# A transformer block on one core: zero products as TensorE warm-up, one weight cast moved to GpSimd, and the first input tile loaded by two queues

## The chip, the core and the metric

The kernel runs on one core of a Trainium2 chip. The metric is the device time of one execution in microseconds (us), the median of several runs. Five engines work side by side, each in the order of its own queue: TensorE (PE, with its weight loads as PEld), VectorE (DVE), ScalarE (ACT), GpSimd (POOL) and SyncE (SP, which here only issues transfers). They wait for each other through semaphores. [...]

## The reference

One pre-LayerNorm transformer block in float32, with S = 2048 tokens, D = 512, 32 heads of 16, and F = 1792:

```
h   = x + A(layernorm(x))
out = h + B(layernorm(h))
A: qkv = x @ wqkv; each token attends to itself and 7 earlier tokens, 2 apart; softmax; @ wo
B: relu(x @ w1 + b1)**2 @ w2 + b2
```

## The kernel before

Matrix products are made in three parts. Every float32 operand is split into a high part (a rounding copy to the type float32r, function `hi`, on ScalarE, or `hi_T` for an activation) and a low part (source minus high part, function `lo`, on VectorE or GpSimd). `mm3` then adds high x high, low x high and high x low in one PSUM bank, 4 k-blocks each, so 12 products.

The first stage makes q, k and v. Tokens come in 16 tiles of 128 rows (`xt`), and the weight matrix `wqkv` in 4 column groups `gp` of 4 row blocks `k` (128x384 each, `wraw` as loaded). The first sixteen slots of the main loop take tiles t = 0 to 3 with each group in turn. Tile t is centred by `x_center` (three VectorE instructions: statistics, their sum, subtraction), transposed by four TensorE instructions (`x_T`, `transposes`, L201), then ScalarE makes its high part `xh` out of PSUM and VectorE its low part `xl` (`lo_T`). In slot t the four high x high products come first, then tile t+1's transposes, then the other eight products (L228). For t = 0 these eight are `xl` by `big_h`, then `xh` by `big_l`; for later tiles the other way round. `big_h` and `big_l` hold the high and low parts of the weights, and `rs` is each row's inverse deviation, which GpSimd makes and ScalarE applies when it copies a result out of PSUM (L526).

The order is written by hand: the kernel schedules nothing by itself. Chores are put down for a slot (`at`, `after`) and emitted there. What stands ahead of the loop is this:

- GpSimd fills the identity matrix `ident` and a few constants (L931 to L937).
- SyncE issues tile 0, tile 1, `wraw` rows k = 2 and 3, tiles 2 and 3 and the other groups; ScalarE issues `wraw` rows k = 0 and 1, since `load_wqkv(0, (0, 1), nc.scalar)` names its queue.
- TensorE transposes `ident` by itself 18 times into a PSUM bank that nobody reads (L949 to L951).
- `x_center(0)`, `x_center(1)`, the high parts of rows k = 0 and 1 on ScalarE (`hi_wqkv`), tile 0's transposes, the high parts of k = 2 and 3, then the low parts: k = 1 and 2 on GpSimd, k = 0 and 3 on VectorE, `x_rstd` on GpSimd, and `x_center(2)`.

After this stage come attention on VectorE and GpSimd, the output projection and the MLP, which the change doesn't touch. `wo_h` holds weights that are first written much later.

## Time and profile before

| what | us |
|---|---|
| median of 3 runs | 504.56 (504.14 to 506.01) |
| the profiled execution, own time | 504.66 |
| its span, first to last instruction | 502.8 |
| TensorE busy in the span | 496.9 (99%) |
| VectorE, ScalarE, GpSimd busy | 378.2, 302.2, 353.4 |

The profiled execution's time is 0.10 us above the median of the runs. Times in the rows count from the span's start. A row of a timeline says start, duration, engine, line, operation, output and inputs, and how many like ones were merged; in brackets stands what the engine waited for. [...]

### The profile page before, as it was taken

How to read it: one execution, taken by the hardware profiler on the slowest of the kernel's cores; microseconds unless marked ns; L12 is line 12 of the kernel's file. 1: busy time of each engine (PE TensorE's matmuls, PEld its weight loads, DVE VectorE, ACT ScalarE, POOL GpSimd, SP SyncE). 2: the span in 40 equal slices, each digit the busy share in tenths (PEclk: the TensorE clock that was granted, in tenths of full speed). 3: DMA queues.
4: the chain of work that ended last, by engine and by line, in shares of the span. 5: the costliest groups of instructions: out<-in, count | busy, mean ns of one | idle time of the engine just before them, and what ended most of it. 6: DMA issues, size and time to landing. Idle time of an engine off the chain costs nothing.

```text
span 502.8 us, 7520 instructions
## 1 busy us (share of the span) xinstructions
PE 496.9 (99%) x2414; PEld 422.6 (84%) x2414; DVE 378.2 (75%) x524; ACT 302.2 (60%) x540; POOL 353.4 (70%) x430
## 2 busy tenths in 40 slices
PE   8999999999999999999999999999999999999997
PEld 7999888888888888888888888888888888998986
DVE  6379899988989989788879998888984255833233
ACT  4635777768346758368564555755554958766541
POOL 5614798886685999969877877769799363786610
PEclk9999999999999999999999999999999999999999
DMA  8678989889798988679576856966654556355112
GB/s 263 188 226 212 315 249 302 285 255 283 219 190 277 303 277 256 201 215 260 179 253 198 222 151 187 234 207 239 219 158 71 127 164 188 112 162 167 64 42 86
DMA packets 111472, 103.15 MB, mean 205 GB/s; under 512 B 31560, under 2 KB 79944, under 8 KB 111432
## 3 DMA queue, kind: packets, MB, share of 16 engines
q1 hardware_dynamic: 110488, 102.14, 69.2%
q10 hardware_dynamic: 944, 0.52, 0.3%
q8 instruction: 19, 0.31, 0.3%
q14 instruction: 21, 0.17, 0.1%
HBM read 72.65 MB, written 24.25 MB: 193 GB/s over the span
## 4 chain that ended last, share of the span: by engine, by line
PE 95%; DVE 1%; issue 1%; POOL 1%; DMA 1%; ACT 0%; POOLq 0%; DVEq 0%
PE mm L228 49%; PE acc L899 28%; PE wo L228 9%; PE mm L822 7%; PE tr L201 2%; DMA xt<-in_A_x_dram 1%; POOL tl L155 1%; DVE s L757 0%; PE half L922 0%; POOL rl L155 0%; POOL h L679 0%; DVE s L758 0%; DVE big_l L155 0%; ACT big_l L152 0%; DVE st L457 0%
## 5 line engine op out<-in xcount | busy, mean ns | idle before, releaser
L408 POOL TENSOR_TENSOR pr<-pr 128x512 f32<-128x512 f32 (+1 forms) x128 | 133.6, 1044 | 35.0 <-DVE pr L351 29.6
L228 PE MATMUL mm<-big_l,w_h 128*128 128x512 f32 x336 | 88.4, 389 | 0.0
L351 DVE TENSOR_TENSOR pr<-ex,v 128x1024 f32<-128x1024 f32 x64 | 78.0, 1220 | 13.7 <-POOL o L408 9.0
L340 DVE TENSOR_TENSOR pr<-qp,k 128x1024 f32<-128x1024 f32 x64 | 76.8, 1200 | 10.7 <-ACT qp L268 7.3
L374 DVE TENSOR_REDUCE ex<-pr 128x64 f32<-128x1024 f32 x64 | 78.5, 1226 | 2.0
L228 PEld LDWEIGHTS mm<-big_l,w_h 128*128 128x128 f32 x336 | 63.0, 188 | 13.4 <-issue 0.3
L155 POOL TENSOR_TENSOR rl<-r,rh 128x512 fp32r<-128x512 f32 x42 | 55.3, 1320 | 25.5 <-ACT rh L152 25.4
L228 PE MATMUL mm<-big_l,xh 128*128 128x512 f32 (+1 forms) x208 | 55.9, 379 | 0.0
L228 PE MATMUL mm<-big_h,xh 128*128 128x512 f32 (+1 forms) x208 | 53.7, 380 | 0.7 <-ACT xh L152 0.7
L228 PE MATMUL mm<-big_h,xl 128*128 128x512 f32 (+1 forms) x208 | 53.0, 377 | 0.0
L899 PE MATMUL acc<-big_h,rh 128*128 128x512 f32 x190 | 52.0, 391 | 0.0
L899 PE MATMUL acc<-big_l,rh 128*128 128x512 f32 x190 | 52.0, 390 | 0.0
L899 PE MATMUL acc<-big_h,rl 128*128 128x512 f32 x190 | 51.7, 389 | 0.0
L228 PE MATMUL mm<-big_l,w_l 128*128 128x512 f32 x168 | 44.9, 389 | 0.0
L228 PEld LDWEIGHTS mm<-big_h,xh 128*128 128x128 f32 x208 | 38.4, 190 | 6.5 <-ACT xh L152 1.1
L228 PEld LDWEIGHTS mm<-big_h,xl 128*128 128x128 f32 x208 | 38.9, 191 | 5.9
L899 PEld LDWEIGHTS acc<-big_h,rl 128*128 128x128 f32 x190 | 35.7, 188 | 7.4
L899 PEld LDWEIGHTS acc<-big_l,rh 128*128 128x128 f32 x190 | 35.6, 188 | 7.5
L228 PEld LDWEIGHTS mm<-big_l,xh 128*128 128x128 f32 x208 | 37.4, 188 | 4.9
L899 PEld LDWEIGHTS acc<-big_h,rh 128*128 128x128 f32 x190 | 35.0, 188 | 6.7
L875 ACT ACTIVATE r<-mm,b_sb 128x512 f32<-128x512 f32 x42 | 28.8, 685 | 15.3 <-PE mm L228 14.6
L528 ACT COPY y<-mm 128x512 f32<-128x512 f32 x36 | 21.1, 586 | 26.7 <-PE mm L228 24.2
(160 smaller groups left out, 918.9 us busy)
## 6 DMA issues: line engine op xcount, KB each, us to landing
k<-qkv_d SPq DMA_DIRECT2D x48, 288.0 KB, 3.6
v<-qkv_d SPq DMA_DIRECT2D x48, 288.0 KB, 3.5
qkv_d<-y SPq DMA_DIRECT2D x18, 512.0 KB, 4.1
big_l<-w2l_d SPq DMA_DIRECT2D x24, 256.0 KB, 3.1
xt<-in_A_x_dram SPq DMA_DIRECT2D x16, 256.0 KB, 4.4
q<-qkv_d SPq DMA_DIRECT2D x32, 128.0 KB, 3.3
h<-in_A_x_dram SPq DMA_DIRECT2D x16, 256.0 KB, 3.6
h_d<-h SPq DMA_DIRECT2D x16, 256.0 KB, 2.8
```

The source lines that it names most:

```text
L155: eng.tensor_tensor(out=dst, in0=src, in1=h, op=ALU.subtract)
L201: nc.tensor.transpose(tr[:, k, :], src[:, k * P:(k + 1) * P], ident)
L228: nc.tensor.matmul(ps, l(k), r(k), start=(n == 0), stop=(n == 3 * KB - 1))
L340: nc.vector.tensor_tensor(out=pr.rearrange("p i w h d -> p i w (h d)"), in0=qps["now"][:, j % 2].unsqueeze(2).to_broadcast([P, RI, W, GC]) ...
L351: nc.vector.tensor_tensor(out=p2, in1=vwin, op=ALU.mult, in0=e1[:, :, :, j * GH:(j + 1) * GH].unsqueeze(4).to_broadcast([P, RI, W, GH, DH]))
L374: nc.vector.tensor_reduce(out=lf[:, :, :, j * GH:(j + 1) * GH], in_=pr, axis=X, op=ALU.add)
L408: nc.gpsimd.tensor_tensor(out=dst, in0=p2[:, :, :w], in1=p2[:, :, w:2 * w], op=ALU.add)
L528: nc.scalar.copy(dst, src)
L822: nc.tensor.matmul(ps, sta[y][:, k], mov[x][:, k], start=(first and q == 0), stop=(last and q == len(terms) - 1), skip_group_check=True)
L875: nc.scalar.activation(r, ps, AF.Relu, bias=b1_sb[:, f:f + 1])
L899: nc.tensor.matmul(acc[j], l[:, j * P:(j + 1) * P], w[f], start=(first and n < len(js)), stop=(last and n >= len(terms) - len(js)))
```

## The change

Four edits, all ahead of the main loop:

1. VectorE fills `blank`, the first 128x128 corner of `wo_h`, with zeros, and TensorE multiplies `blank` by itself 21 times (float32r, 128 columns) in place of the 18 transposes of `ident`.
2. Three more such products stand between tile 0's transposes and its first real product.
3. The high part of weight row k = 1 of group 0 is made by GpSimd.
4. Tile 0 is loaded as two transfers of 64 rows, one issued by SyncE, one by ScalarE ahead of its two weight rows.

```
-WARM = 18
+WARM = 21, 3
...
-    def hi_wqkv(gp, k):
-        hi(pair(wq_h, k, gp), raws[gp, k])
+    def hi_wqkv(gp, k, copy=nc.scalar.copy):
+        copy(pair(wq_h, k, gp), raws[gp, k])
...
+    blank = wo_h[:, 0, :P]
+    nc.vector.memset(blank.bitcast(F32), 0.0)
     make_identity(nc, ident)
...
-    load_x(0)
+    xt[0] = row("xt")
+    for n, eng in enumerate((nc.sync, nc.scalar)):
+        half = slice(n * P // 2, (n + 1) * P // 2)
+        eng.dma_start(xt[0][half], x_v[0, 0, 0, half])
     load_wqkv(0, (0, 1), nc.scalar)
...
-    for n in range(WARM):
-        nc.tensor.transpose(warm[:, n % KB, :], ident, ident)
+    def keep_busy(count):
+        for n in range(count):
+            nc.tensor.matmul(warm[:, n % KB, :], blank, blank, start=True, stop=True)
+
+    keep_busy(WARM[0])
...
     hi_wqkv(0, 0)
-    hi_wqkv(0, 1)
+    hi_wqkv(0, 1, nc.gpsimd.tensor_copy)
...
     x_T(0)
+    keep_busy(WARM[1])
     run(due)
```

On TensorE, from its first instruction to the first product, the order changes so (- before, + now; `tr` is the PSUM bank, `mm` the first product's bank):

```order
-L951 MATMUL tr<-ident 128x128 x18
-L201 MATMUL tr<-ident,xt 128x128 x4
+L958 MATMUL tr<-wo_h 128x128 x21
+L201 MATMUL tr<-ident,xt 128x128 x4
+L958 MATMUL tr<-wo_h 128x128 x3
 L228 MATMUL mm<-big_h,xh 128x384 x4
```

The warm-up is of another kind, and three of it stand behind the transposes; nothing else moves on TensorE in the whole program.

On ScalarE, before, from its first transfer to the casts behind tile 0's `xh`:

```order
L562 DMA wraw<-in_A_wqkv_dram 128x3x128 x2
L152 ACT_TABLE_LOAD
L152 CAST big_h<-wraw 128x3x128 x2
L152 CAST xh<-tr 128x512
L152 CAST big_h<-wraw 128x3x128 x2
```

And now:

```order
L944 DMA xt<-in_A_x_dram 64x512
L562 DMA wraw<-in_A_wqkv_dram 128x3x128 x2
L565 ACT_TABLE_LOAD
L565 CAST big_h<-wraw 128x3x128
L152 CAST xh<-tr 128x512
L565 CAST big_h<-wraw 128x3x128 x2
```

One transfer has come in ahead of the weight rows, and one cast of a weight row instead of two stands ahead of `xh`.

On GpSimd, behind the constants, now:

```order
L938 AFFINE_SELECT mask<-mask 128x32
L565 CAST big_h<-wraw 128x3x128
L155 TENSOR_TENSOR big_l<-wraw,big_h 128x3x128 x2
L465 TENSOR_SCALAR rs_154<-mv_153 128x1
L467 TENSOR_TENSOR rs_154<-rs_154,mhalf 128x1
```

The cast is new there; before, the two low parts (L155) followed the mask directly.

## Rows read from the trace of the kernel before

**Rows 1.** Waits of PE in the whole span: us in total, times, longest.
```profile
PE mm L228 <- ACT xh L152: 0.7, 1, 0.7
PE mm L822 <- DVE wo_l L155: 0.5, 1, 0.5
```
**Rows 2.** The chain that ended last, first 30 us: start, us, what.
```profile
0.72 3.40 DMA xt<-in_A_x_dram
...
4.15 0.70 DVE st L457
...
6.79 0.59 ACT xh L152
...
7.42 1.65 PE mm L228 x4
9.07 0.85 PE tr L201 x4
...
12.45 0.44 PE tr L201 x4
```
**Rows 3.** Timeline of PEld, first 16 us.
```profile
1.34 3.71 PEld L951 LDWEIGHTS tr<-ident 128*128 128x128 f32 x18 [1.34 <-POOL ident masks.py:199]
...
9.51 1.19 PEld L228 LDWEIGHTS mm<-big_h,xl 128*128 128x128 f32 x4
10.69 0.71 PEld L228 LDWEIGHTS mm<-big_l,xh 128*128 128x128 f32 x4
```
**Rows 4.** Timeline of PE, first 16 us.
```profile
5.63 1.11 PE L201 MATMUL tr<-ident,xt 128*128 128x128 f32 x4 [0.19 <-DVE xt L459]
...
8.87 1.05 PE L201 MATMUL tr<-ident,xt 128*128 128x128 f32 x4
...
11.57 0.87 PE L228 MATMUL mm<-big_h,xh 128*128 128x384 f32 x4
12.28 0.60 PE L201 MATMUL tr<-ident,xt 128*128 128x128 f32 x4
```
**Rows 5.** Timeline of ACT, first 16 us.
```profile
5.30 1.15 ACT L152 CAST big_h<-wraw 128x384 fp32r<-128x384 f32 x2 [1.96 <-DMA wraw<-in_A_wqkv_dram]
6.79 0.59 ACT L152 CAST xh<-tr 128x512 fp32r<-128x512 f32 x1 [0.34 <-PE tr L201]
7.27 0.93 ACT L152 CAST big_h<-wraw 128x384 fp32r<-128x384 f32 x2
```
**Rows 6.** Timeline of SP, first 16 us: its issues of transfers.
```profile
0.72 0.87 SPq L439 DMA_DIRECT2D xt<-in_A_x_dram  x2
1.64 1.34 SPq L562 DMA_DIRECT2D wraw<-in_A_wqkv_dram  x2
```
**Rows 7.** Transfers, first 20 us: issues, KB each, median us to landing.
```profile
wraw<-in_A_wqkv_dram SPq DMA_DIRECT2D x14, 192.0 KB, 4.3
```
**Rows 8.** Transfer queues (q1 SyncE's, q10 ScalarE's), 2.4 to 2.9 us: packets, MB, share.
```profile
q1 hardware_dynamic: 34, 0.06, 57.6%
q10 hardware_dynamic: 2, 0.00, 0.6%
```
**Rows 9.** Timeline of POOL, first 16 us: two low parts of weight rows.
```profile
6.53 2.33 POOL L155 TENSOR_TENSOR big_l<-wraw,big_h 128x384 fp32r<-128x384 f32 x2 [4.75 <-DMA wraw<-in_A_wqkv_dram]
```
**Rows 10.** Timeline of DVE, first 20 us.
```profile
8.01 1.74 DVE L155 TENSOR_TENSOR big_l<-wraw,big_h 128x384 fp32r<-128x384 f32 x2
9.67 0.68 DVE L457 BATCH_NORM_STATS2 st<-xt 128x6 f32<-128x512 f32 x1
...
10.60 0.49 DVE L459 TENSOR_SCALAR xt<-xt,mv 128x512 f32<-128x512 f32 x1
```
**Rows 11.** Timeline of DVE, 16 to 20 us: a low part alone.
```profile
16.69 0.55 DVE L155 TENSOR_TENSOR big_l<-wraw,big_h 128x384 fp32r<-128x384 f32 x1
```
**Rows 12.** Groups of POOL by shape, first 20 us: busy us, mean ns of one.
```profile
L155 POOL TENSOR_TENSOR big_l<-wraw,big_h 128x384 fp32r<-128x384 f32 x8 | 8.6, 1083 | 5.3 <-DMA wraw<-in_A_wqkv_dram 4.7 <-ACT big_h L152 0.4
...
masks.py:199 POOL TENSOR_SCALAR_AFFINE_SELECT ident<-ident 128x128 f32<-128x128 f32 x1 | 0.3, 292 | 0.1
...
masks.py:197 POOL MEMSET ident<- 128x128 f32 x1 | 0.2, 204 | 0.3 <-POOLq L1246 0.3
...
L933 POOL MEMSET mhalf<- 128x1 f32 x1 | 0.1, 98 | 0.0
```

## The prediction

> **What bounds the kernel now.** I read TensorE's waits first. Behind its start-up TensorE waits once in 500 us, 0.5 us at L822 near 427 us, and that wait hangs on work that TensorE itself feeds [rows 1]. So TensorE's queue is the span, and what the change can win lies ahead of the point where that queue runs without a break. The chain shows what stands there: tile 0's transfer (0.72 to 4.12), its centring (from 4.15), its transposes, its `xh` on ScalarE (6.79), then products from 7.42 [rows 2].

> The second thing is the rate. The weight loads of four 384-column products take 1.19 us from 9.51 and 0.71 us from 10.69 [rows 3]; four transposes take 0.85 in the chain at 9.07 and 0.44 at 12.45 [rows 2]. [...] (The page's clock line reads full speed in all slices; the distances decide.) A 384-column product thus costs 0.30 us at the low level (1.19/4) and 0.18 at the high one (0.71/4).

> Three marks serve below, each a start on TensorE: tile 1's transposes at 8.87, slot 1 at 11.57, and tile 2's transposes at 12.28 [rows 4].

> **The change, part by part.**

> *Warm-up.* VectorE is idle at the start; its memset should take about what GpSimd's of the same size does, 0.20 [rows 12]; from 0.72, where the other queues begin [rows 2, 6], TensorE starts near 0.95, not 1.34. No row shows a 128-column float32r product. Bounds at the low level: 0.10 each, if it went by columns as the 384-column ones do (0.30/3), and 0.43, twice a warm-up transpose. I take a transpose's 0.21 (3.71/18 [rows 3]), which has the same columns and the same size of weight load. 21 of them end at 5.4, or near 4.9 if the clock rises on the way. [...] The three later products (0.33 at the high level, 0.64 at the low) fit in the 0.68 between the transposes' end (6.74) and the first product (7.42), in which ScalarE makes `xh` [rows 2, 4], so I cost them nothing; without that cover they would cost those 0.33.

> *Tile 0 in halves.* Landing lies between 3.1 (SyncE's queue had the engines nearly alone until 2.9 [rows 8], and half the bytes remain on it) and today's 4.12. I take 3.5. Centring costs 1.48 as now (4.15 to 5.63), so the transposes can start near 5.0 to 5.4, and end by 5.6 to 6.1.

> [...]

> *ScalarE.* `xh` stands behind the cast of weight row k = 0, which starts when that row lands, 5.30 now [rows 5]. Its issue slips behind the half tile's, by at most 0.43 (0.87/2 [rows 6]); I take 5.5. With one cast gone, `xh` follows one cast spacing later (0.48, as 6.79 to 7.27 [rows 5]): 5.98, and the first product 0.63 after that, at 6.6 instead of 7.42. So the earlier tile is worth little beyond this: ScalarE's weight row is late next.

> *GpSimd's cast.* Row k = 1 could start at 5.94 now (5.30 + 1.15 - 0.51 [rows 5]); with the slip 6.14. Price: at least ScalarE's 0.51 for the same tile, at most GpSimd's two-input 1.08 [rows 12]. I take 0.68: from 0.098 for one column and 0.292 for 128 (AFFINE_SELECT), three times the difference plus 0.098 [rows 12]. Ready at 6.9, as its product is due at 6.8: 0.1 lost.

> *Row k = 3.* ScalarE casts it last. It lands between 6.6 (second issue near 2.3 [rows 6] plus the median 4.3 [rows 7]) and 7.68, where its cast began unhindered. With 7.2 it is ready at 7.75; its product follows and tile 1's transposes start at 7.93 instead of 8.87. Gain so far 0.94. At the high clock the transposes and the four `xl` products then take 0.44 + 0.70, to 9.1.

> *The low parts.* Now comes what the moved cast pushes. GpSimd's two low parts started at 6.53 [rows 9]; behind the cast they start at 6.9. VectorE's two took 1.74 together from 8.01, where one alone takes 0.55 [rows 10, 11]: the first could only finish after GpSimd's second had ended at 8.86. The two engines hold each other up here, so four low parts come nearly in a row: GpSimd to 7.9, VectorE to 8.35, then one of each, the last ready between 9.4 and 9.8. Slot 1 starts at 9.8 to 10.0 instead of 11.57. But tile 2's centring stands behind VectorE's second low part and lasts 1.42 (9.67 to 11.09 [rows 10]). If VectorE goes ahead of GpSimd at 8.35, it is done at 10.2, and TensorE, due at 10.6, waits for nothing: gain 1.7. If GpSimd goes first, it is done at 11.2: tile 2's transposes start at 11.25, gain 1.0. I take 1.2.

> [...]

> *Sum.* 0.94 up to tile 1's transposes, 0.8 more by the clock up to slot 1, some 0.5 given back at tile 2's transposes: about 1.2. Behind these TensorE's queue has no wait that a shift makes longer, and ScalarE and GpSimd are pulled along with some slack; so the gain should reach the end. From the profiled execution's 504.66 that gives 503.46, from the median, 0.10 lower, 503.36.

> **The rivals.**

> A. *The clock is still low.* Products with zeros may not count as work, or the pause before `xh` may undo it. If the level rises at 10.69 as now, the first four products from 6.6 take to 8.05 (the last waits for k = 3), the transposes to 8.9, the next four to 10.1, the last four, two at each level, to 11.05: gain 0.5 at slot 1 and at tile 2, about 504.1. For it: 18 transposes did nothing visible. [...] No run here shows zeros. Chance 0.15.

> B. *No hold-up.* Row k = 3 lands early (6.8), VectorE goes first. Then only the stream counts: tile 1's transposes at 7.5, slot 1 near 9.4: gain 2.1, 502.5. Chance 0.15.

> C. *The weights are what is late.* The half tile on ScalarE's queue and the shared engines put rows 0 and 1 back by 0.6 or more: `xh` at 6.4, k = 1 ready at 7.5, and the low parts behind it all as late: gain 0.4, 504.2. Likewise if a later wait that rows don't show takes the gain back. Chance 0.12.

> D. *The warm-up outlasts its cover.* At 0.43 each and the low level throughout, 21 products end at 9.95, and tile 0's transposes, ready near 5.0, stand behind them. From there TensorE needs at the least 4.1 to slot 1 (0.6 transposes, 0.68 `xh`, 1.0 first four with ScalarE's casts, 0.44, 0.7, 0.7 at the high level), so slot 1 is at 14.05: 2.5 later than now, 507.1. It decides from 0.31 each, where 0.95 + 21 x 0.31 + 4.1 is 11.57. Against it: 384 columns of the same type cost 0.30 at the low level, so 128 should hardly cost more. Chance 0.04.

> **How the numbers follow.** The forecast, gain 1.0 to 1.7, has 0.54. The prediction is 503.4. For eight in ten I take in the forecast, A, B and C, from 502.4 to 504.5; beyond lie D and what scatter between runs adds. Half a per cent, 2.5 us, is about what a measurement of this kernel can tell from no change, and no case on the good side reaches it: faster 0.02, within 0.94, slower 0.04.

> **What would show it.** Right: the four first products' weight loads come 0.18 apart (or wait singly for a cast), tile 0's `xh` starts near 6.0, tile 1's transposes near 7.9, tile 2's near 11, and TensorE's later waits are as now. GpSimd's cast shows its price, and VectorE's low parts show who held whom up. Wrong: loads 0.3 apart after 6.6 (A), the warm-up's products further apart than 0.25 (D), slot 1 before 9.6 (B), or a new wait after 20 us.

## The result and the profile after

The change is slower: 506.45 us (505.42 to 507.33, 10 runs) against 504.41 (503.71 to 506.01, 10 runs), a ratio of 1.0039 with a 95% interval of 1.0027 to 1.005. That is 2.0 us more, and inside the 0.5% that the prediction counted as no change. The profiled execution took 506.59 us, with a span of 504.8.

TensorE's waits in the profile after (engine, operation and line, what it waited for: us in total, times, longest):

```profile
PE tr L958 <- DVE wo_h L933: 1.0, 1, 1.0
PE mm L228 <- DVE xl L155: 0.7, 1, 0.7
PE mm L822 <- DVE wo_l L155: 0.5, 1, 0.5
```

The warm-up begins at 1.0 instead of 1.3, the wait at L822 is as it was [rows 1], and there is a new one, for an `xl` of VectorE. The timeline of TensorE's weight loads after (start us, us, engine, line, operation, count) answers to [rows 3]:

```profile
1.04 4.55 PEld L958 LDWEIGHTS tr<-wo_h 128*128 128x128 f32 x21 [1.04 <-DVE wo_h L933]
5.92 0.71 PEld L201 LDWEIGHTS tr<-ident,xt 128*128 128x128 f32 x4 [0.33 <-issue]
6.62 0.76 PEld L958 LDWEIGHTS tr<-wo_h 128*128 128x128 f32 x3
7.71 1.14 PEld L228 LDWEIGHTS mm<-big_h,xh 128*128 128x128 f32 x4 [0.33 <-ACT xh L152]
...
9.79 1.19 PEld L228 LDWEIGHTS mm<-big_h,xl 128*128 128x128 f32 x4
10.97 1.29 PEld L228 LDWEIGHTS mm<-big_l,xh 128*128 128x128 f32 x4
12.26 0.77 PEld L228 LDWEIGHTS mm<-big_h,xh 128*128 128x128 f32 x4
```

The 21 products on zeros stand 0.22 apart (4.55/21), but the real products behind them come 0.30 apart (1.19/4) until 12.26. The trace's record of the granted clock begins at 12.38, at full speed (1.0); in the trace of before it begins at 10.69. The warm-up filled the time, and no rise came before the first product. The first product is at 7.71 (7.42 before) and, in the timeline of TensorE, slot 1 at 12.49 (11.57).

ScalarE, SyncE, GpSimd and VectorE in the same stretch, each in its timeline after (they answer to [rows 5, 6, 9, 10]; a q behind the engine's name marks an issue of a transfer):

```profile
0.72 0.60 ACTq L944 DMA_DIRECT2D xt<-in_A_x_dram  x1
1.35 1.37 ACTq L562 DMA_DIRECT2D wraw<-in_A_wqkv_dram  x2
...
5.54 0.51 ACT L565 CAST big_h<-wraw 128x384 fp32r<-128x384 f32 x1 [1.51 <-DMA wraw<-in_A_wqkv_dram]
7.07 0.59 ACT L152 CAST xh<-tr 128x512 fp32r<-128x512 f32 x1 [1.02 <-PE tr L201]
```

```profile
0.73 0.59 SPq L944 DMA_DIRECT2D xt<-in_A_x_dram  x1
1.38 0.56 SPq L439 DMA_DIRECT2D xt<-in_A_x_dram  x1
```

```profile
7.33 0.50 POOL L565 CAST big_h<-wraw 128x384 fp32r<-128x384 f32 x1 [5.54 <-DMA wraw<-in_A_wqkv_dram]
7.92 2.28 POOL L155 TENSOR_TENSOR big_l<-wraw,big_h 128x384 fp32r<-128x384 f32 x2
```

```profile
4.42 0.69 DVE L457 BATCH_NORM_STATS2 st<-xt 128x6 f32<-128x512 f32 x1 [3.43 <-DMA xt<-in_A_x_dram]
...
8.30 2.31 DVE L155 TENSOR_TENSOR big_l<-wraw,big_h 128x384 fp32r<-128x384 f32 x2
10.53 0.68 DVE L457 BATCH_NORM_STATS2 st<-xt 128x6 f32<-128x512 f32 x1
```

Each half of tile 0 took 0.6 us to issue, and the tile's statistics start at 4.42 instead of 4.15. Row k = 1 is late: GpSimd waits for it to 7.33. No product waits for it, though: it is cast by 7.83, and the second product is due 0.29 behind the first (1.14/4), at 8.0. With the low parts behind it VectorE comes to tile 2 at 10.53 (9.67 before).

Much later stands the new wait. The chain of work after, 62 to 66 us (start us, us, what):

```profile
62.34 1.23 DVE pr L351
63.57 0.02 issue
63.59 1.23 DVE ex L374
64.82 0.60 DVE xl L155
...
65.46 2.58 PE mm L228 x10
```

There VectorE, not TensorE, is the chain, in the middle of attention work. Its timeline leads back to tile 4, first in the trace after, then in that of before:

```profile
32.89 0.69 DVE L163 BATCH_NORM_STATS2 st<-xt 128x6 f32<-128x512 f32 x1 [3.34 <-DMA xt<-in_A_x_dram]
```

```profile
31.09 0.69 DVE L163 BATCH_NORM_STATS2 st<-xt 128x6 f32<-128x512 f32 x1 [2.43 <-DMA xt<-in_A_x_dram]
```

VectorE stands idle until tile 4 lands, 1.8 later than before. Before, the same `xl` ended at 63.31, 0.45 us ahead of the product that needs it, by the timelines of VectorE and TensorE:

```profile
62.63 0.68 DVE L155 TENSOR_TENSOR xl<-tr,xh 128x512 fp32r<-128x512 f32 x1
```

```profile
63.76 1.07 PE L228 MATMUL mm<-big_h,xl 128*128 128x512 f32 x4
```

In the change nothing of that is left. From tile 4's landing to the `xl` at 64 VectorE is busy 29.1 of 31.7 us, as the busy times by stretch have it (us from and to, length, then busy us and count of PE, PEld, DVE, ACT and POOL, granted clock, DMA share, GB/s); its one wait there is 1.8 us for GpSimd (1.5 before):

```profile
33.00:64.70 31.70, 31.70 (x164) 28.06 (x162) 29.08 (x43) 18.42 (x41) 17.46 (x27) 1.00 0.85 238
```

So the 2.0 us of the profiles' spans (504.8 against 502.8) come as 0.9 up to slot 1, 1.0 at 64 to 66 us (0.8 of it the wait itself), and 0.3 at 329 us (another wait for a low part), of which 0.2 is won back by 375 us. Of the 0.9, 0.3 is there at the first product. The rest comes from the products at 10.97, which still run at the low level and take 1.29 us, where those at 10.69 took 0.71 before [rows 3].

### The profile page after: what moved, and what is told of

Its sections match the earlier page's. It is cut to its first block, busy times and chain, and to the rows that moved or that the text cites. A ratio compares the mean times of both kernels' runs of the same rounds, so it can differ in the third digit from the quotient of the medians.

```text
span 504.8 us, 7536 instructions
## 1 busy us (share of the span) xinstructions
PE 499.1 (99%) x2420; PEld 424.8 (84%) x2420; DVE 382.3 (76%) x525; ACT 301.4 (60%) x539; POOL 354.5 (70%) x431
## 4 chain that ended last, share of the span: by engine, by line
PE 83%; DVE 2%; issue 1%; POOL 1%; ACT 0%; POOLq 0%; DVEq 0%
PE mm L228 38%; PE acc L899 28%; PE wo L228 9%; PE mm L822 7%; PE tr L201 2%; POOL tl L155 1%; DVE s L757 0%; PE half L922 0%; POOL rl L155 0%; POOL h L679 0%; DVE pr L351 0%; DVE ex L374 0%; DVE s L758 0%; DVE big_l L155 0%; ACT big_l L152 0%
## 5 line engine op out<-in xcount | busy, mean ns | idle before, releaser
L155 POOL TENSOR_TENSOR rl<-r,rh 128x512 fp32r<-128x512 f32 x42 | 55.3, 1321 | 25.4 <-ACT rh L152 25.3
L228 PEld LDWEIGHTS mm<-big_l,w_l 128*128 128x128 f32 x168 | 31.5, 188 | 6.6
```

What stands on the lines that cost most here:

```text
L155: eng.tensor_tensor(out=dst, in0=src, in1=h, op=ALU.subtract)
L228: nc.tensor.matmul(ps, l(k), r(k), start=(n == 0), stop=(n == 3 * KB - 1))
```

## The experiments

Times are medians against the runs of the kernel before made beside them. The medians of those were 504.43 (e1 to e4), 504.35 (e7 to e10), 504.09 (e5, e11 to e13), 504.29 (e14 to e17) and 504.13 (e18, e19). A kernel ran 12 times, but the change 10 times, e3 and e18 9 times, and e7 and e19 6 times. "Full clock from" is where the trace's record of the granted clock begins, with 1.0 of full speed, or rises to it from 0.5; the distances of the weight loads agree. (The views print 1.00 for the time before the record begins.)

| run | us | ratio, 95% interval | full clock from | slot 1 |
|---|---|---|---|---|
| before | 504.41 | | 10.69 | 11.57 |
| after | 506.45 | 1.0039, 1.0027 to 1.005 | 12.38 | 12.49 |
| e1_zeros_only | 505.45 | 1.0021, 1.0006 to 1.0035 | 12.0 | 12.26 |
| e2_cast_only | 504.17 | 0.9995, 0.9983 to 1.0007 | 10.53 | 11.50 |
| e3_split_only | 505.89 | 1.0033, 1.0016 to 1.0049 | 13.46 | 13.02 |
| e4_no_split | 505.30 | 1.0016, 1.0007 to 1.0026 | 9.41 | 11.03 |
| e7_no_warmup | 507.46 | 1.0059, 1.0036 to 1.0083 | 11.98 | 12.40 |
| e8_ones | 505.84 | 1.0027, 1.0016 to 1.0038 | 10.34 | 11.38 |
| e9_wide | 505.13 | 1.0017, 1.0002 to 1.0033 | 4.88 | 10.11 |
| e10_wide_ones | 504.94 | 1.0015, 1.0001 to 1.0028 | 4.46 | 10.00 |
| e5_no_zeros | 506.39 | 1.0040, 1.0022 to 1.0058 | 13.79 | 12.80 |
| e11_x4_early | 503.37 | 0.9986, 0.9973 to 0.9998 | 5.02 | 10.05 |
| e12_wide_x4_early | 504.62 | 1.0008, 0.9995 to 1.0022 | 7.35 | 10.57 |
| e13_change_x4_early | 505.71 | 1.0031, 1.0016 to 1.0046 | 12.32 | 12.53 |
| e14_x4_zeros | 505.09 | 1.0010, 0.9996 to 1.0024 | 11.58 | 11.95 |
| e15_x4_split | 506.04 | 1.0026, 1.0012 to 1.0040 | 14.02 | 13.37 |
| e16_x4_cast | 503.60 | 0.9988, 0.9973 to 1.0003 | 6.55 | 10.45 |
| e17_x4_nowarm | 504.96 | 1.0004, 0.9992 to 1.0016 | 11.45 | 11.92 |
| e18_x4_split_cols | 506.05 | 1.0032, 1.0016 to 1.0048 | 6.50, lost at 9.92, again 13.33 | 13.59 |
| e19_x4_split_pool | 507.86 | 1.0072, 1.0049 to 1.0095 | 6.01, lost at 9.42, again 12.84 | 13.91 |

### Each part alone, on the kernel before

e1, the warm-up alone (its memset, 21 products and 3 behind tile 0's transposes):

```
-    for n in range(WARM):
-        nc.tensor.transpose(warm[:, n % KB, :], ident, ident)
+    keep_busy(WARM[0])
```

> The kernel before with the warm-up of the change alone (21 + 3 products of zeros). Theory Z (products of zeros do not lift the clock): the first real product starts at 7.4 as before, its weight loads are 0.32 apart, and the higher level comes somewhere between 10 and 12.5, so the time is that of before plus 0 to 0.7. Theory W (zeros do lift it, and in the change something else spoilt it): loads 0.18 apart from the first product on, slot 1 before 10.7, time 1 us less than before.

e2, the cast alone, and e3, the split alone:

```
-    hi_wqkv(0, 1)
+    hi_wqkv(0, 1, nc.gpsimd.tensor_copy)
```

> The kernel before with weight row k = 1 cast by GpSimd, nothing else. Theory P (the moved cast is what holds VectorE's low parts up): VectorE's two low parts take 2.3 together instead of 1.74, tile 2's centring begins 0.5 later than in the kernel before, but its transposes still have 0.6 to spare, so slot 1 moves by 0.1 at most, and the time by 0 to 0.3. Theory Q (the cast frees ScalarE): tile 0's xh starts at 6.5 instead of 6.79 and the time falls by 0.2. If a stall near 64 us stands in this run too, the cast alone makes it.

```
-    load_x(0)
+    xt[0] = row("xt")
+    for n, eng in enumerate((nc.sync, nc.scalar)):
+        half = slice(n * P // 2, (n + 1) * P // 2)
+        eng.dma_start(xt[0][half], x_v[0, 0, 0, half])
```

> The kernel before with tile 0 in two halves, nothing else. Theory S (the split makes the tile later): VectorE's first statistics start near 4.4 instead of 4.15, ScalarE's second weight row lands near 7.2 instead of 5.9, and since its cast stands ahead of tile 0's xh on ScalarE here, xh waits for it: first product near 8.5, time 1 us more than before. Rival (the split is harmless, the delay in the change is scatter of the transfers): statistics at 4.1, row k = 1 at 6.0, time as before.

e4, the change without the split:

```
-    xt[0] = row("xt")
-    for n, eng in enumerate((nc.sync, nc.scalar)):
...
+    load_x(0)
```

> The change without the split of tile 0. Theory S: first product near 7.4 again, row k = 1 cast by GpSimd from 5.95, low parts 0.6 earlier than in the change; time 0.3 to 1 us less than the change. If the clock is what counts (theory Z), the loads are still 0.32 apart until 10 to 12.5 and the time is between before and the change. If the stall near 64 us comes from the split, it is gone here.

Zeros alone cost 1.0 us and the split alone 1.5, both more than expected; the cast costs nothing that can be measured (-0.3). The sum, 2.2, is near the change's 2.0. Without its split (e4) the change is 0.9 above before, so in the change the split is worth some 1.2. In e2 neither theory's detail came true: VectorE's two low parts took 1.73 together, as before, and `xh` started at 6.79, as before. But the traces show waits at other places each time: 0.95 at 381 us in e1, 0.73 at 229 us in e2, none in e4. With one trace of each, single parts could not yet be priced.

### What the warm-up is worth

e7 has no warm-up; in e8 the narrow products are on ones; in e9 they are 10 + 1 products of 512 columns on zeros, and in e10 the same on ones:

```
-    for n in range(WARM):
-        nc.tensor.transpose(warm[:, n % KB, :], ident, ident)
```

> The kernel before without any warm-up: the 18 transposes are left out (their results are read by nobody). Theory V (no warm-up of either kind moves the clock, and the spread from 9.4 to 13.5 of the moment it rises is chance): first product at 7.4, the rise at 9 to 13.5, the time that of before within 0.5. Rival (the 18 transposes do bring the rise forward, and zeros do so less): the rise later than 11, the time 0.5 to 1.5 above before.

```
-    nc.vector.memset(blank.bitcast(F32), 0.0)
+    nc.vector.memset(blank.bitcast(F32), 1.0)
```

> The kernel before with the warm-up of the change on ones in place of zeros. Theory N (zeros don't count because nothing switches): with ones the products of tile 0 run 0.18 apart from the first, the time falls by about 1 below before. Rival (this kind of warm-up, 128 columns behind each weight load, does not lift the clock whatever it multiplies): as with zeros, the rise after 9.4, the time 0.5 to 1.5 above before.

```
-            nc.tensor.matmul(warm[:, n % KB, :], blank, blank, start=True, stop=True)
+            nc.tensor.matmul(warm, blank, wide.rearrange("p (k c) -> p k c", k=KB), start=True, stop=True)
```

> The kernel before with a warm-up of products of zeros 512 columns wide, 10 ahead of tile 0's transposes and 1 behind them. Theory D (what TensorE does between weight loads matters: products that follow each other without a gap in the columns lift the clock, on zeros too): the higher level before 7.4, slot 1 near 10.3, the time about 1.2 below before. Rival N (zeros don't count): the rise after 9.4 as with narrow zeros, the time at or above before.

```
-    nc.vector.memset(wide.bitcast(F32), 0.0)
+    nc.vector.memset(wide.bitcast(F32), 1.0)
```

> As the run with wide zeros, on ones. Theories D and N both say that the clock is up before 7.4 here and slot 1 near 10.3, the time about 1.2 below before; if it isn't, no warm-up of this length lifts it and theory V stands. D and N part in the run with wide zeros.

What lies in the operand made no difference in these traces: with narrow ones the clock was not up at the first product, as with narrow zeros (first product at 7.33, full clock from 10.34 in e8), and wide zeros did as well as wide ones. With the 512 columns the clock is up at 4.5 to 4.9, and slot 1 starts at 10.0 to 10.1, as the prediction wanted it. The weight loads in e9:

```profile
7.16 0.60 PEld L228 LDWEIGHTS mm<-big_h,xh 128*128 128x128 f32 x3 [0.75 <-ACT xh L152]
...
9.24 0.71 PEld L228 LDWEIGHTS mm<-big_l,xh 128*128 128x128 f32 x4
```

And yet both end 0.6 to 0.8 us slower than before, where 1.2 faster was expected. e9's TensorE waits say where the gain of 1.5 us went:

```profile
PE mm L228 <- DVE xl L155: 1.1, 1, 1.1
PE wo L228 <- DVE ol L155: 0.6, 1, 0.6
```

The first stands at 62 us, the `xl` that also stops the change, the second at 380 us. At both TensorE was there ahead of VectorE's low part, by 1.1 and 0.6. e7, with no warm-up at all, is 3.1 us above its runs of before, more than either side expected; in its trace TensorE waits 0.8 for an `xl` near 65 us and 0.3 near 36 us.

### The second chain: tile 4

e11 is the kernel before with tiles 4 and 5 loaded two slots earlier; e12 adds e9's wide products, e13 is the whole change with the same edit. e5 is the change with the old warm-up, without the edit:

```
-        if n in (5, 6, 12, 14):
-            at(0, load_x, n - 1 if n < 7 else n // 2)
+        if n in (3, 4, 12, 14):
+            at(0, load_x, n + 1 if n < 7 else n // 2)
```

> The kernel before with the loads of tiles 4 and 5 put down two slots earlier, so that SyncE issues them ahead of the k, q and v loads instead of behind them. Theory M (a second chain bounds the kernel: tile 4's load lands late behind the k and v loads, VectorE waits for it near 31 us, and TensorE waits for VectorE's xl near 64): VectorE's statistics of tile 4 come 2 us earlier, its xl near 64 is ready over 1.5 before TensorE needs it instead of 0.45, no stall there; time 0.3 to 1 below before, since the stall strikes in some runs of before too. Rival (the stall near 64 is chance of another kind): xl and the time as before.

> The warm-up with wide zeros, which had the clock up before the first product and gave its gain back at 62 us, with tiles 4 and 5 loaded earlier as well. Theory M: the stall at 62 is gone and slot 1 is near 10.1, so the gain of 1.3 stays at least until 380, and the time is 0.8 to 1.5 below before. Rival (a later wait, near 380, takes it in any case): TensorE waits there for 1 to 2, the time as before or above.

> The change with tiles 4 and 5 loaded earlier. Theory M: what the change loses behind 60 us (0.8 of its 2.0) is gone, what it loses in the first 13 us stays: time 0.5 to 1.3 above before. If all of the 2.0 stays, the loss is not where the trace of the change put it.

```
-    keep_busy(WARM[0])
+    for n in range(WARM):
+        nc.tensor.transpose(warm[:, n % KB, :], ident, ident)
...
-    keep_busy(WARM[1])
```

> The change without its warm-up, with the 18 transposes of before: the split and the moved cast remain. If the split costs what it cost alone (1.6), the time is 1 to 1.8 above before; the difference to the change is then what the products of zeros cost against the transposes, which theory V puts at 0 and the run with zeros alone at 1.

e5, the change with the old warm-up put back, is 2.3 us above its runs of before, more than the 1 to 1.8 expected and no better than the change: with the split in, the transposes win nothing back, and in e5's trace the clock rose only at 13.79.

e11 has the lowest median of the study, 503.37, 0.7 us below its runs of before, and 11 of its 12 runs lie within 0.54 us (the twelfth is 504.69), where the 35 of before are spread over 3.3. Its VectorE timeline shows tile 4 in place in time, with no wait in front:

```profile
28.17 0.68 DVE L163 BATCH_NORM_STATS2 st<-xt 128x6 f32<-128x512 f32 x1
```

No wait at 62 to 66 us is left in e11, e12 or e13, nor in the six later traces with this edit; of the eleven without it, five have one (after, e7, e8, e9, e10). So that wait hangs on tile 4's landing. e12 still loses its lead, at 379 us, and ends 0.5 above its runs of before, as the rival had it. Its chain there:

```profile
375.01 3.03 DMA v<-qkv_d
...
379.27 1.17 DVE ol L155
380.44 0.04 issue
380.49 1.19 PE wo L228 x4
```

Again a transfer paces VectorE, and VectorE holds TensorE. And e13 shows that the wait at 64 us was not the main loss: without it the change still costs 2.3 us against e11, and 1.6 against its runs of before, where 0.5 to 1.3 was expected.

e11's edit comes into effect only behind 15 us, so its first 12 us are those of the kernel before once more. Its weight loads, against [rows 3]:

```profile
1.34 3.70 PEld L951 LDWEIGHTS tr<-ident 128*128 128x128 f32 x18 [1.34 <-POOL ident masks.py:199]
5.33 0.42 PEld L201 LDWEIGHTS tr<-ident,xt 128*128 128x128 f32 x4 [0.29 <-DVE xt L459]
7.11 0.60 PEld L228 LDWEIGHTS mm<-big_h,xh 128*128 128x128 f32 x3 [1.35 <-ACT xh L152]
...
8.54 0.65 PEld L228 LDWEIGHTS mm<-big_h,xl 128*128 128x128 f32 x4
```

Tile 0's four transposes come 0.11 apart here, where the profiled execution of before had 0.18: the clock was up at 5.02, and the 18 transposes were all that TensorE had done. It was up by 6.6 in four of the nine traces with these transposes. TensorE's lead over the profile of before, 1.3 us at the end, is there by 16 us, ahead of anything that e11's edit touches; the edit kept it from being lost at 64 us. How much of the 0.7 us is the edit's own is not shown.

### The parts again, on the quieter base

The four runs below all have e11's edit; e14 adds e1's, e15 e3's, e16 e2's, e17 e7's.

```
+    keep_busy(WARM[0])
...
         if n in (3, 4, 12, 14):
             at(0, load_x, n + 1 if n < 7 else n // 2)
```

> The kernel with tiles 4 and 5 loaded earlier (503.37 us), with the change's products on zeros in place of the 18 transposes. Theory 1 (the transposes lift the clock in the early stretch, narrow zeros don't): the clock rises after 9 us, slot 1 starts at 11 to 12.3 instead of 10.05, no stall at 64, about 504.3 to 505. Rival (the zeros cost only through the stall near 64): 503.2 to 503.7, slot 1 below 10.5.

```
+        eng.dma_start(xt[0][half], x_v[0, 0, 0, half])
...
         if n in (3, 4, 12, 14):
```

> Tiles 4 and 5 loaded earlier, and the first tile in two halves, nothing else. Theory 1 (the split's price is in the start: issues of 0.60 us, weight rows and tile later): tile 0's statistics start 0.3 or more later than 3.85, first product 0.3 to 1.0 later than 7.11, no stall at 64, 504 to 505. Rival (its price was the stall near 64): 503.2 to 503.7.

```
+    hi_wqkv(0, 1, nc.gpsimd.tensor_copy)
...
         if n in (3, 4, 12, 14):
```

> Tiles 4 and 5 loaded earlier, and GpSimd's cast of row k=1, nothing else. Theory 1 (the cast is neutral: it frees ScalarE but the low parts follow it): 503.1 to 503.7, GpSimd's cast takes 0.50. Rival (worth what ScalarE's cast took, 0.5): 502.6 to 503.0, with the first product at 6.6.

```
-        nc.tensor.transpose(warm[:, n % KB, :], ident, ident)
...
         if n in (3, 4, 12, 14):
```

> Tiles 4 and 5 loaded earlier, and no warm-up on TensorE at all. Theory 1 (the transposes are what brings the clock up early): the clock rises after 11 us, slot 1 at 12 or later, no stall at 64, 504.7 to 506. Rival (the warm-up does nothing, the 3.1 us without it were the stalls): 503.2 to 503.8.

Against e11's 503.37, zeros cost 1.7 and no warm-up at all 1.6 us. (The two were timed beside runs of before that were 0.2 higher than e11's, so 1.5 and 1.4 are as fair; against e16, timed beside them, it is 1.5 and 1.4 too.) All of e11's runs but one lie below the fastest of either (504.66 and 504.37), so this is not the profiled execution's alone. The weight loads of e14, then of e17:

```profile
9.48 1.19 PEld L228 LDWEIGHTS mm<-big_h,xl 128*128 128x128 f32 x4
10.66 1.14 PEld L228 LDWEIGHTS mm<-big_l,xh 128*128 128x128 f32 x4
11.78 0.71 PEld L228 LDWEIGHTS mm<-big_h,xh 128*128 128x128 f32 x4
```

```profile
9.53 1.19 PEld L228 LDWEIGHTS mm<-big_h,xl 128*128 128x128 f32 x4
10.71 1.05 PEld L228 LDWEIGHTS mm<-big_l,xh 128*128 128x128 f32 x4
11.75 0.71 PEld L228 LDWEIGHTS mm<-big_h,xh 128*128 128x128 f32 x4
```

They are alike: 21 narrow zero products did what no warm-up did (full clock from 11.58 and from 11.45). Theory 1 holds in both, with small misses (505.09 for at most 505, slot 1 at 11.92 for 12); the rivals' times are off by 1.2 and more. The cast is neutral, at 503.60 (0.50 us on GpSimd, as expected).

The split costs 2.7 us here (some 2 by the ratios, 1.0026 and 0.9986), more than either side expected. The first product comes at 8.51, 1.4 later than in e11, and ScalarE's timeline in e15 shows what it hangs on:

```profile
5.76 0.51 ACT L152 CAST big_h<-wraw 128x384 fp32r<-128x384 f32 x1 [1.81 <-DMA wraw<-in_A_wqkv_dram]
7.46 0.51 ACT L152 CAST big_h<-wraw 128x384 fp32r<-128x384 f32 x1 [1.19 <-DMA wraw<-in_A_wqkv_dram]
7.88 0.58 ACT L152 CAST xh<-tr 128x512 fp32r<-128x512 f32 x1
```

Row k = 1, behind the half tile on ScalarE's queue, lands at 7.46 (6.06 in e11), and tile 0's `xh` stands behind its cast. The tile alone would have had `xh` some 0.9 later than e11, since its statistics start at 4.74 (3.85 in e11). The change's move of that cast to GpSimd takes `xh` out of this queue (7.07 in the profile after, first product 7.71). That fits the whole change being no slower than its split alone: e13 ends at 505.71, with its first product at 7.83. In e15 the clock rose only at 14.0, and in the two other traces with split and transposes at 13.5 and 13.8 (e3, e5): none of the three was lifted early. So a part of the split's price here is the early clock that e11 had.

### Why the split is late

e18 splits tile 0 by columns in place of rows, e19 gives the second half of the rows to GpSimd's queue; both have e11's edit:

```
+    for n, eng in enumerate((nc.sync, nc.scalar)):
+        half = slice(n * D // 2, (n + 1) * D // 2)
+        eng.dma_start(xt[0][:, half], x_v[0, 0, 0][:, half])
```

> Tiles 4 and 5 loaded earlier; the first tile in halves of its columns (128 rows by 256 columns each) by the same two queues. If the form of the halves is the cost: each issue takes 0.40 to 0.45, tile 0's statistics start at 3.9 or earlier, first product near 7.2, 503.2 to 504.2. If ScalarE's queue is the cost: its weight rows land later all the same, first product at 7.6 or later, 505 or more.

```
-    for n, eng in enumerate((nc.sync, nc.scalar)):
+    for n, eng in enumerate((nc.sync, nc.gpsimd)):
```

> Tiles 4 and 5 loaded earlier; the first tile in halves of its rows, the second by GpSimd's queue in place of ScalarE's. If ScalarE's queue is the cost: weight rows k=0 and k=1 land as in the kernel before (casts at 5.3 and 5.9), first product at 7.4 or earlier, 503.2 to 504.2. If the form of the halves is the cost: tile 0's statistics still start at 4.4 or later, first product 7.7 or later, 504.8 or more. GpSimd's issue may itself be slower, which its row shows.

By columns an issue takes 0.39 and 0.42, not 0.6, and tile 0's statistics start at 3.68. In the thirteen traces with the whole tile they start at 3.85 to 4.52, in the five with the halves by rows on these two queues at 4.42 to 4.89. The form of the halves is thus what made the tile itself late, as far as one trace shows it. Yet the run is as slow as e15: on ScalarE's queue the weight row is late all the same.

```profile
5.28 0.51 ACT L152 CAST big_h<-wraw 128x384 fp32r<-128x384 f32 x1 [1.50 <-DMA wraw<-in_A_wqkv_dram]
8.02 0.51 ACT L152 CAST big_h<-wraw 128x384 fp32r<-128x384 f32 x1 [2.23 <-DMA wraw<-in_A_wqkv_dram]
8.44 0.58 ACT L152 CAST xh<-tr 128x512 fp32r<-128x512 f32 x1
```

Row k = 1 lands at 8.02, and TensorE stands still for 3.2 us with tile 0 long transposed. In that trace the clock had been up from 6.5, behind the transposes, and the busy times by stretch (columns as above) show it lost again:

```profile
7.40:9.50 2.10, 0.43 (x2) 0.31 (x3) 0.45 (x1) 1.48 (x4) 0.89 (x1) 1.00 1.08 347
9.50:11.50 2.00, 2.00 (x9) 1.70 (x8) 2.00 (x4) 0.37 (x2) 1.83 (x4) 0.60 0.97 285
11.50:13.50 2.00, 2.00 (x8) 2.00 (x8) 1.93 (x5) 1.38 (x3) 1.83 (x5) 0.54 0.91 262
```

After the stretch in which TensorE stood still, the granted clock is at half from 9.92 to 13.33, and TensorE has all the work it can do in that time. It is not this execution's alone: all nine runs of e18 have a mean granted clock of 0.993 to 0.997, and so have four of six of e19, five of nine of e3 and three of twelve each of e5 and e15, where the change's ten have 0.999 to 1.0. If that is the same drop, the clock was up early in some executions with the split too, and was lost again; the traces of e3, e5 and e15 show none.

e19 misses as a test of ScalarE's queue. GpSimd's issue began at 1.75 and took 0.76, its half landed so late that tile 0's statistics start at 7.07, and TensorE waited 3.1 us for it. ScalarE's queue was free of the half, and row k = 0 came earlier (4.63), but k = 1 later (6.61). It shows only that the half came later by GpSimd's queue than by ScalarE's (statistics at 7.07, against 4.42 to 4.89).

## Why the prediction was wrong

I forecast 503.4 us and a range to 504.5; the time is 506.45. The step that failed first is the clock: the sum has all real products at the high level's price from the first on, 0.18 each. No run shows that from the first product on behind a warm-up of narrow products. In the profile after, the real products come 0.30 apart, and the full clock starts at 12.38. In six traces with narrow products as warm-up (after, e1, e4, e8, e13, e14) the clock is low at the first product each time (1.14 to 1.21 for the weight loads of four); in three with 512 columns (e9, e10, e12) it is high each time (0.60 for those of three). My price for a product was right (0.21 taken, 0.22 measured), and so was its cover. Against the profile of before the later rise makes 0.6 of the 0.9 us at slot 1. Rival A had this case, but it took the old warm-up for worthless ("18 transposes did nothing visible"), from one profiled execution. In four of nine traces with the transposes (e11, e16, e18, e19) the clock was up by 6.6. So the change gave up something that neither my sum nor rival A had as a cost: some 1.5 us where tile 0 comes in time, as e17 and e14 against e11 show. That is no share of the change's 2.0, though. With the split in, the transposes win nothing back (e5), so the losses by zeros and by split overlap; by how much is open.

In these four traces transposes were all that TensorE had done before the rise, in e11 the 18 alone. All four have e11's edit, and the four traces with transposes but without it rose late; since that edit touches nothing before 15 us, no cause is shown in this. What decides between one execution and another, and why 128-column products fared worse, stays open.

The second failed step is tile 0's landing, "I take 3.5", between 3.1 and 4.12: the statistics start at 4.42. The upper bound was false, since it took the issue of a half to cost no more than that of the whole (0.4); it cost 0.6. By halves of columns, issued in 0.39 and 0.42, the statistics started at 3.68 in e18, 0.17 below the earliest of the thirteen traces with the whole tile, which scatter by 0.67; in the change nothing was saved.

Third, row k = 1, "with the slip 6.14", came at 7.33. I had the weight rows slip by their issue alone. For k = 0 the time came true (5.5 forecast, 5.54 measured), though its issue slipped by 0.63 where I had at most 0.43. For k = 1 the issue slipped by 0.69, to 2.08, and the landing by 1.39. Rival C had the mechanism ("k = 1 ready at 7.5"; it was at 7.83), but still as a gain. In the profile after no product waited for k = 1, so this miss cost nothing there. The first product, at 7.71 instead of the forecast 6.6, hangs on tile 0: `xh` waited 1.02 us for its transposes, which ran from 5.92, at the low clock, and started at 7.07 instead of 5.98. Slot 1 is at 12.49 instead of 9.8 to 10.0.

What hung on GpSimd came out nearly as said. Its cast took 0.50, below my 0.68 and at my lower bound. GpSimd's two low parts ran from 7.92 to 10.20, VectorE's two from 8.30 to 10.61, 2.31 together where one alone takes 0.55 [rows 11]: VectorE's second ended 0.4 behind GpSimd's. I had that case, GpSimd first, in the range.

The last failed step is "Behind these TensorE's queue has no wait that a shift makes longer", so that "the gain should reach the end". The list of waits in the profile before shows only waits that happened. `xl` at 63 us ended 0.45 us before TensorE came to it, and no row of that list can show this slack. So a second bound was there: tile 4's landing, then VectorE to 64 us. In the change that wait cost 0.8 us. And e9 and e10 show that the forecast would have failed with its mechanism working too: a lead of 1.5 us at slot 1 was gone by the end. With tile 4 moved the lead reached the end in e11 and e16; in e12 it was lost at 379 us. In e9, e10 and e11 the lead behind tile 2's transposes was 1.2 to 1.3 us, the 1.2 of my sum, but with neither split nor moved cast: that the sizes meet is chance.

## What to carry to other kernels

Judge a warm-up by the distances of the real instructions behind it, in several executions, before replacing it: one profile showed the old one as idle, and where the tile came in time it was worth about 1.5 us. A transfer split over two queues pushed back what stood behind it on both (in the profile after, the issues of the weight rows start at 1.98 instead of 1.64 on SyncE's queue, at 1.35 instead of 0.72 on ScalarE's); look for the next consumer there before counting the tile's own gain. And before a gain at the start is carried to the end, look on the other engines for work that ends just ahead of TensorE and is paced by a transfer. Such slack is in no list of waits; here moving two loads by two slots (e11) left no wait at 64 us in nine traces, with a median 0.7 us lower.
